# A packed-attention and SMeLU kernel on one core: casting loads, DMA transposes, no GpSimd compute, small matmuls on array tiles

## The chip, the cores and the metric

One core of one Trainium2 chip. The metric is the device time of one execution in microseconds. Times of kernels are medians of their runs. Stage times come from the trace of one profiled execution, counted from the start of its span, which is a little shorter than the timed run.

Engines: PE is TensorE (PEld its weight loads), DVE is VectorE, ACT is ScalarE, POOL is GpSimd, SP is SyncE.

## The reference

Eight batches (B) of eight heads (H), 576 tokens (S), head size 64 (D), 32 packing tokens per head. Cut to what matters:

```python
def sm_attn(qq, kk, vv):                       # softmax attention, scale 1/8
    ...
p_packed = sm_attn(p, k, v)                    # 32 packed rows per head
x = sm_attn(q, p_packed, p_packed)             # every token attends to 32 rows
x = x.transpose(0, 2, 1, 3).reshape(B * S, H * D)          # 4608 x 512
h = x @ w_in                                   # 512 x 2048
g = where(h >= 1, h, where(h <= -1, 0, (h + 1)**2 / 4))    # SMeLU
out = g @ w_out                                # 2048 x 512, float32
```

Both kernels use the same algebra: the second attention times `w_in` is regrouped as probabilities `A` times `M`, where `M` is the packed values times `w_in`.

## The kernel before

Each batch goes through: load k, v, q as float32; cast to bf16; transpose k and q on TensorE; scores, packed values, `M`, `A`; then a *stage* of 16 hidden tiles (`h`), into which the attention of the next batch, the output tiles (`o`) of the batch before and the casts of a later batch are woven. A scheduler orders the instructions of each engine.

```python
def load_tokens(src, b, tag, eng):             # float32, 4 tokens per partition, the rest apart
    t = stg.tile([P, H, NC4, D], f32, tag=tag, name=tag)          # one buffer per tensor
    eng.dma_start(...)
    r = stg.tile([REM, H, D], f32, tag=tag + "r", name=tag + "r")
    eng.dma_start(...)
...
def cast_steps(nm, b, engs): ...               # four casts per tensor, on the engines given
...
def scores(c0, n):                             # keys of two heads on all 128 rows,
    ... nc.tensor.matmul(sp[:, c, hp], kT[:, hp, ...], pT_blk[:, b, hp]...)   # p block-diagonal
...
def mk(g, f):                                  # M, on the whole array
    mp = psA.tile([P, FW], f32, tag="a", name="mp")
    for j in range(2):
        nc.tensor.matmul(mp, ppT[:, g, j], w_in_sb[:, 2 * g + j, ...], start=(j == 0), stop=(j == 1))
...
def hidden_tile(b, fi):
    ... # 4 matmuls of 288 columns into h
    nc.scalar.activation(r, hv, AF.Relu, bias=half, scale=0.5)
    if (fi * PB_SHARE) % 8 < PB_SHARE:         # 10 of 16 tiles
        nc.gpsimd.tensor_mul(u, r, r)
    else:
        nc.scalar.activation(u, r, AF.Square)
    nc.vector.scalar_tensor_tensor(dst, u, 1.0, hv, ALU.min, ALU.max)
...
run(cast_steps("k", 0, (V, A_, G_)))           # V, A_, G_: VectorE, ScalarE, GpSimd
...
for n in "kvq":
    run(cast_steps(n, 1, (V, A_, G_)))
```

The softmax here doesn't subtract the row's maximum and nothing guards it: scores larger than these inputs give would overflow.

## Time and profile before

334.59 us, median of 3 runs (333.87 to 337.23). From the trace, counted at the first matmul of `h` of each batch:

| stretch | us |
|---|---|
| start, to the first `h` | 37.1 |
| stage of batch 0 | 43.7 |
| stage of batch 1 | 31.0 |
| stages of batches 2 to 6 | 173.9 (34.8 each) |
| stage of batch 7, to the end of its last `h` | 26.7 |
| tail: the last output tiles | 21.6 |

First the page of the kernel before: busy time of TensorE; busy tenths of TensorE, of GpSimd and the granted TensorE clock in tenths of full speed, each in 40 equal slices of the span; and the shares of the chain that ended last.

```profile
PE 282.1 (84%) x1879; PEld 164.9 (49%) x1912; DVE 180.3 (54%) x324; ACT 206.7 (62%) x371; POOL 162.2 (49%) x190
...
PE   0274868887878998999899999999999999988894
...
POOL 4092237599858849237824693242433242434300
PEclk9998599997999999999999999999999999999999
...
PE 34%; issue 17%; POOL 16%; DMA 11%; DVE 10%; ACT 10%; POOLq 0%; SPq 0%; ACTq 0%
```

In the first thirteen slices (of 8.35 us each) TensorE never reaches 9 tenths, and GpSimd is at 8 or 9 tenths in five of the slices 9 to 14. The chain has 16% of GpSimd in it and 17% of "issue", so TensorE does not bound the whole run. Next, waits of the kernel before (engine, line, what was waited for: us in total, times, longest).

```profile
DVE hT L301 <- POOL u L298: 80.3, 66, 3.4
...
ACT kb_129 L125 <- DMA k<-in_k_dram: 8.6, 1, 8.6
...
DVE kb_129 L127 <- DMA k<-in_k_dram: 3.8, 1, 3.8
```

The last step of the hidden tiles (`hT`, on VectorE) waits 80 us in all for squares on GpSimd. ACT and VectorE each stand still once for a cast of batch 1's keys, which have not landed.

Last, pieces of TensorE's timeline of the kernel before (start, us, then what, and how many were merged). The last matmul of a group overlaps the first of the next, so the cost of a group is the difference of two starts, not the second column.

```profile
217.37 1.24 PE L321 MATMUL o<-w_out_sb,hT 128*128 128x512 bf16 x5
218.45 0.65 PE L288 MATMUL h<-A,M 128*128 128x288 bf16 x4
218.94 0.61 PE L166 MATMUL tp<-ident,kb_121 128*128 128x128 bf16 x8
...
221.19 0.40 PE L193 MATMUL sp<-pT_blk,kT 128*128 128x64 bf16 x8
221.64 0.81 PE L321 MATMUL o<-w_out_sb,hT 128*128 128x512 bf16 x3
...
228.52 0.84 PE L207 MATMUL pp<-vb_125,ex 128*128 128x320 bf16 x5
229.20 1.03 PE L321 MATMUL o<-w_out_sb,hT 128*128 128x512 bf16 x4
```

Five output matmuls take 1.08 us, 0.216 each; four of `h` 0.49. Eight scores (`sp`) take 0.45 here, but the next eight only 0.23 and the last four 0.12. Five packed matmuls (`pp`) take 0.68.

### The profile page before, as it was taken

What the parts mean: (1) busy time and instruction counts of PE and PEld (TensorE: products, weight loads), DVE (VectorE), ACT (ScalarE), POOL (GpSimd) and SP (SyncE); (2) the same over time, 40 slices, a digit from 0 to 9 for tenths busy, and PEclk for the clock granted to TensorE, in tenths of its full rate; (3) what the DMA queues carried; (4) which work ended last, traced back from release to release, by engine and by line L of the source; (5) the groups of instructions that cost most, each with busy time, mean ns of one, the idle gap of its engine ahead of it and who ended that gap; (6) DMA issues with size and microseconds to landing.
All of it is one profiled execution on the core that took longest, in us unless ns stands there. A gap on an engine that the chain in (4) does not pass through costs nothing.

```text
span 334.0 us, 5198 instructions
## 1 busy us (share of the span) xinstructions
PE 282.1 (84%) x1879; PEld 164.9 (49%) x1912; DVE 180.3 (54%) x324; ACT 206.7 (62%) x371; POOL 162.2 (49%) x190
## 2 busy tenths in 40 slices
PE   0274868887878998999899999999999999988894
PEld 0152345455444565557454655566546655444441
DVE  5332477564637764486457653767476638444300
ACT  2123745964668765966597747866977588666411
POOL 4092237599858849237824693242433242434300
PEclk9998599997999999999999999999999999999999
DMA  8999994577599595915740200000001200010031
GB/s 215 252 236 310 230 260 150 159 200 210 152 271 253 117 295 163 260 59 154 210 140 31 59 34 31 31 33 33 31 31 37 60 33 32 31 64 32 31 96 63
DMA packets 41689, 42.54 MB, mean 127 GB/s; under 512 B 12800, under 2 KB 35328, under 8 KB 41664
## 3 DMA queue, kind: packets, MB, share of 16 engines
q1 hardware_dynamic: 33472, 30.68, 31.6%
q0 software_dynamic: 8192, 11.54, 16.0%
q8 instruction: 15, 0.25, 0.3%
q14 instruction: 10, 0.08, 0.1%
HBM read 37.22 MB, written 9.44 MB: 140 GB/s over the span
## 4 chain that ended last, share of the span: by engine, by line
PE 34%; issue 17%; POOL 16%; DMA 11%; DVE 10%; ACT 10%; POOLq 0%; SPq 0%; ACTq 0%
PE o L321 15%; POOL u L298 9%; PE h L288 8%; DVE hT L301 5%; ACT r L295 4%; DMA kr<-in_k_dram 4%; PE mp L259 4%; DMA q<-in_q_dram 3%; DMA k<-in_k_dram 3%; DVE M L264 2%; PE tp L166 2%; DVE A L254 2%; ACT u L300 2%; POOL qb_131 L127 2%; POOL kb_121 L127 1%
## 5 line engine op out<-in xcount | busy, mean ns | idle before, releaser
L298 POOL TENSOR_TENSOR u<-r 128x576 f32<-128x576 f32 x80 | 91.7, 1148 | 126.8 <-ACT r L295 117.7
L301 DVE SCALAR_TENSOR_TENSOR hT<-u,h 128x576 bf16<-128x576 f32 x128 | 96.2, 752 | 94.7 <-POOL u L298 80.3
L321 PE MATMUL o<-w_out_sb,hT 128*128 128x512 bf16 x549 | 141.8, 380 | 1.5
L295 ACT ACTIVATE r<-h,half 128x576 f32<-128x576 f32 x128 | 94.7, 741 | 69.7 <-PE h L288 67.0
L288 PE MATMUL h<-A,M 128*128 128x288 bf16 x512 | 85.1, 290 | 16.0 <-DVE hT L301 15.4
L321 PEld LDWEIGHTS <-hT 128*128 128x128 bf16 x576 | 54.6, 98 | 49.8 <-DVE hT L301 0.6
L288 PEld LDWEIGHTS <-M 128*128 128x128 bf16 x512 | 49.5, 98 | 56.1 <-issue 20.6
L259 PE MATMUL mp<-w_in_sb,ppT 128*128 128x512 bf16 x122 | 36.9, 391 | 5.2 <-DVE M L264 3.1
L325 ACT COPY ob<-o 128x512 f32<-128x512 f32 x36 | 21.1, 587 | 20.2 <-PE o L321 20.0
L300 ACT ACTIVATE u<-r 128x576 f32<-128x576 f32 x48 | 32.9, 686 | 0.5
L264 DVE CAST M<-mp 128x512 bf16<-128x512 f32 x32 | 21.3, 684 | 9.1 <-PE mp L259 9.0
L254 DVE TENSOR_TENSOR A<-eT,rc 128x288 bf16<-128x288 bf16 x32 | 20.1, 632 | 6.3 <-ACT rc L253 6.2
L259 PEld LDWEIGHTS <-ppT 128*128 128x128 bf16 x128 | 12.8, 100 | 16.3 <-issue 10.6
L262 ACT CAST M<-mp 128x512 bf16<-128x512 f32 x32 | 18.7, 583 | 1.9 <-PE mp L259 1.6
L195 ACT ACTIVATE ex<-sp 128x512 bf16<-128x512 f32 (+1 forms) x24 | 12.3, 518 | 7.3 <-PE sp L193 7.2
L253 ACT ACTIVATE rc<-ln 128x288 f32<-128x288 f32 x32 | 14.1, 446 | 0.6
L167 DVE COPY qT<-tp 128x1024 bf16<-128x1024 bf16 x16 | 11.0, 688 | 4.8 <-PE tp L166 4.5
L251 ACT ACTIVATE ln<-sm 128x288 f32<-128x288 f32 x32 | 13.0, 411 | 0.1
L167 DVE COPY kT<-tp 128x1024 bf16<-128x1024 bf16 x16 | 11.0, 686 | 0.6 <-PE tp L166 0.4
L166 PE MATMUL tp<-ident,kb_121 128*128 128x128 bf16 x64 | 5.9, 242 | 6.2 <-DVE pT_blk L153 6.2
L193 PE MATMUL sp<-pT_blk,kT 128*128 128x64 bf16 x160 | 9.7, 200 | 0.9 <-ACT ex L195 0.6
L207 PEld LDWEIGHTS <-ex 128*128 128x128 bf16 x80 | 8.3, 104 | 3.7 <-issue 0.7
(152 smaller groups left out, 237.1 us busy)
## 6 DMA issues: line engine op xcount, KB each, us to landing
out_dram<-ob SPq DMA_DIRECT2D x32, 256.0 KB, 2.3
k<-in_k_dram SPq DMA_DIRECT2D x6, 1024.0 KB, 7.1
v<-in_v_dram SPq DMA_DIRECT2D x6, 1024.0 KB, 8.4
q<-in_q_dram SPq DMA_DIRECT2D x6, 1024.0 KB, 8.3
w_in_sb<-in_moe_w_in_dram POOLq DMA_DIRECT2D x4, 512.0 KB, 8.3
k<-in_k_dram POOLq DMA_DIRECT2D x2, 1024.0 KB, 9.5
v<-in_v_dram POOLq DMA_DIRECT2D x2, 1024.0 KB, 8.8
q<-in_q_dram POOLq DMA_DIRECT2D x2, 1024.0 KB, 9.9
```

Of the source, the lines that this page charges most:

```text
L167: nc.vector.tensor_copy(T[:, :, base + c0 * P:base + (c0 + 2) * P], tp.rearrange("p h c t -> p h (c t)"))
L254: nc.vector.tensor_mul(A[:, g, hf * HALF:(hf + 1) * HALF], eT, rc)
L259: nc.tensor.matmul(mp, ppT[:, g, j], w_in_sb[:, 2 * g + j, f * FW:(f + 1) * FW], start=(j == 0), stop=(j == 1))
L262: nc.scalar.copy(M[:, g, f * FW:(f + 1) * FW], mp)
L264: nc.vector.tensor_copy(M[:, g, f * FW:(f + 1) * FW], mp)
L288: nc.tensor.matmul(h[:, hf, :HALF], M[:, g, fi * P:(fi + 1) * P], A[:, g, hf * HALF:(hf + 1) * HALF], start=(g == 0), stop=(g == G - 1))
L295: nc.scalar.activation(r, hv, AF.Relu, bias=half, scale=0.5)
L298: nc.gpsimd.tensor_mul(u, r, r)
L300: nc.scalar.activation(u, r, AF.Square)
L301: nc.vector.scalar_tensor_tensor(dst, u, 1.0, hv, ALU.min, ALU.max)
L321: nc.tensor.matmul(o, hT[:, fi, i * P:(i + 1) * P], w_out_sb[:, fi, :], start=(fi == 0), stop=(fi == KF - 1))
L325: nc.scalar.copy(ob, o)
```

## The change

The intent is to free GpSimd and the casts' share of the other engines, and to take work off TensorE. Its parts:

1. Tokens are loaded by DMAs issued from GpSimd that cast float32 to bf16 on the way, six tokens on each of 96 partitions.
2. From batch 3 on, keys and queries are transposed by the DMA, SBUF to SBUF; before that on TensorE. One transpose turns two neighbouring chunks of a head: even chunks land on rows 0 to 63, odd ones on rows 64 to 127 (chunk parity).
3. Scores, packed values, probabilities and `M` run as many small matmuls on tiles of the array (64x96, 96x64, 64x32), instead of fewer ones on all of it with zero blocks.
4. The activation is a leaky ramp on ACT, a second pass on ACT or VectorE in turn, and a product on VectorE. GpSimd computes nothing but the identity matrix.
5. One pool of three two-bank buffers in PSUM (the memory that matmuls write to) for all but the output tiles, an order made by hand, and 25 matmuls on zeros at the start, meant to hold the clock.

```diff
 def load(nm, b):
+    t = stg.tile([TP, H, NC, D], bf16, tag=nm, name=nm)           # TP 96, NC 6, two buffers
+    nc.gpsimd.dma_start(t.rearrange("p h c d -> p h (c d)"), ...[b].rearrange("h (p c) d -> p h (c d)", c=NC))
...
+def xbar(b):
+    for nm, T in zip("kq", keys(b)):
+        nc.sync.dma_start_transpose(T.rearrange("p h e t -> p (h e) t"), tok[nm, b].rearrange("p h c d -> p (h c d)"))
...
 def scores(e0, n):
+    for e in range(n):
+        for g in range(G):
+            for a in range(Q):
+                for x in range(X):                                # row half = chunk parity
+                    r = slice(x * D, (x + 1) * D)
+                    nc.tensor.matmul(sp[:TP, x, e, g, a], kT[r, G * a + g, e0 + e], pT[r, b, g, a], ...)
...
 def mk(f):
+    for a in range(Q):
+        for g in range(G):
+            r = slice(g * D, (g + 1) * D)
+            nc.tensor.matmul(mp[a * NP:(a + 1) * NP, g], ppT[r, g, a], w_in_sb[r, a, ...], start=True, stop=True)
...
 def hidden_tile(b, fi, kind):
-    nc.scalar.activation(r, hv, AF.Relu, bias=half, scale=0.5)
-    ... nc.gpsimd.tensor_mul(u, r, r) / nc.scalar.activation(u, r, AF.Square) ...
-    nc.vector.scalar_tensor_tensor(dst, u, 1.0, hv, ALU.min, ALU.max)
+    nc.scalar.activation(x, hv, AF.Prelu, bias=-1.0, alpha=0.5)
+    # kind "W": nc.scalar.activation(t, x, AF.Relu, bias=1.0)
+    # kind "V": nc.vector.tensor_scalar(t, x, 1.0, 0.0, ALU.add, ALU.max)
+    nc.vector.scalar_tensor_tensor(dst, t, 1.0, t, ALU.min, ALU.mult)
...
+            a[26].append(lambda b=b: xbar(b + 2))                 # slot 26 of the 32 of a stage
```

## The prediction

> **What bounds the kernel now** (timeline, first matmul of `h` per batch).
> (a) 0 to 37 us: no hidden tile yet. TensorE is 11, 29 and 55% busy in the three ten-us windows from 0; casts wait for loads (8.6 us on ACT for one k in the waits view), and the granted clock falls to 0.50 in 30 to 40 us.
> (b) batch 0, 37 to 81 us: 43.7 us; GpSimd is 87% busy in 60 to 80 us with casts (1.04 us each) and squares (1.15 us, 80 of them); the chain of waits runs through both (POOL 16%).
> (c) batches 1 to 6, 81 to 286 us: 34.2 us each. TensorE is the limit: 97 to 99% busy in 200 to 280 us.
> (d) batch 7 (27 us) and the last five output tiles (21.5 us), nearly all TensorE.
>
> **TensorE per batch, before**, from start-to-start times in the timeline: 72 output matmuls at 0.216 = 15.5; 64 hidden at 0.122 = 7.8; 16 for `M` at 0.216 = 3.5; 40 transposes at 0.056 = 2.2; packed 1.4 plus 0.2; probabilities and sums 1.5; 20 scores at 0.033 = 0.7. Sum 32.8.
>
> **What the change does there.** Output and hidden matmuls (23.3 us) stay. `M` becomes 32 matmuls on 64-by-32 tiles, eight at a time. The Trainium skill ("TensorE: Matmul & The Clock Gate", Part 3) says such tiles run concurrently; not shown here yet. Estimate 1.3 us, saving 2.1. Probabilities likewise save 0.6. Transposes leave TensorE from batch 3 on, saving 2.2. But scores grow from 20 to 48 matmuls and packed from 10 to 48 plus 12, none with a full 128-column weight load: estimate 40 to 55 ns each, so 4.5 to 5 against 2.3. "TensorEngine Tiling (Array Packing)", Key Properties, says that changing the tiling mode drains the engine; about 20 changes per batch, estimate 1 to 2 us. Net: about 31.5 us, only 1 to 2 us less per batch.
>
> **Other engines.** ACT per batch: 16 first passes (0.74), 8 second passes (0.69), evacuations near 10: 27.6 as before, so 85% of the stage. VectorE 20 to 22. GpSimd computes nothing. ACT and TensorE now share three two-bank PSUM buffers; estimate 1 to 2 us of stalls per stage.
>
> **Where the gain lies.** Mostly in (a) and (b). No casts stand between landing and transposes, warming matmuls hold the clock: first `h` at about 26 us (saves 11), set by the first half of w_in behind k, v, q at 250 to 300 GB/s. Batch 0 stage 28 to 30 us (saves 14), set by ACT. Batch 1 about 34 (waiting for w_out and the third batch's q, around 66 to 73 us). Batches 2 to 6 about 32.5 each. Batch 7 24, tail 21.5.
> Sum: 26 + 29 + 34 + 162 + 24 + 21.5 = 296.5; I lean lower, as the placement looks tuned.
>
> **Predicted: 294 us, 8 in 10 between 276 and 312. Faster by over 2%: 0.90; within: 0.07; slower: 0.03.**
>
> **Right if** the profile shows: first `h` before 29 us; batch 0 under 32 us; no compute on POOL; steady stages 31 to 33 us with TensorE above 90% busy; eight `M` matmuls starting within about 0.4 us.
>
> **Wrong if**: the DMA transposes (590 KB each, issued about 9 us before the scores need them) take over 9 us, stalling every batch from 3 on (up to +30 us); small matmuls cost 80 ns each (+2 us per batch); mode changes cost more than 0.15 us; ACT, 85% loaded and in order, locks step with TensorE and becomes the limit; or tiles do not overlap, so `M` costs 6.9 us.

## More of the kernel before

Now the windows view, one stage per line (from and to, length; busy us and instructions of each engine; granted clock, DMA share, GB/s): batch 0, then batch 4.

```profile
37.06:80.76 43.70, 35.12 (x254) 20.63 (x258) 26.92 (x47) 27.58 (x48) 29.33 (x38) 0.93 0.83 208
182.37:218.45 36.08, 34.72 (x243) 20.73 (x246) 21.59 (x37) 25.08 (x47) 19.70 (x23) 1.00 0.11 37
```

In batch 4's stage TensorE is busy 34.7 of 36.1 us; in batch 0's, 35.1 of 43.7.

## The result, and the profile after

283.38 us, median of 4 runs (282.4 to 284.23), against 334.45 us for the kernel before in the same rounds. The ratio is 0.8459 (95% interval 0.841 to 0.8508). Ratios here are the mean time of one kernel's fast runs over that of the other's of the same rounds, so not quite the ratio of the medians quoted. A run more than 1.5% above the fastest of its kernel counts as slow and is left out of the ratios.

By stretch, from the two traces:

| stretch | before | predicted | after | after less before |
|---|---|---|---|---|
| start, to the first `h` | 37.1 | 26 | 24.7 | -12.4 |
| batch 0 | 43.7 | 29 | 28.7 | -15.0 |
| batch 1 | 31.0 | 34 | 32.7 | +1.7 |
| batches 2 to 6 | 173.9 | 162 | 150.8 | -23.2 |
| batch 7 | 26.7 | 24 | 21.0 | -5.7 |
| tail | 21.6 | 21.5 | 22.8 | +1.2 |
| span | 334.0 | 296.5 | 280.6 | -53.4 |

The page of the changed kernel, the same lines:

```profile
PE 257.3 (92%) x2545; PEld 142.1 (51%) x2545; DVE 175.9 (63%) x305; ACT 196.9 (70%) x309; POOL 27.1 (10%) x42
...
PE   6696885899999999989999999799999999999992
...
POOL 8411107002101200011001200000000000000000
PEclk9968899599999999999999999999999999999998
...
PE 70%; DVE 10%; DMA 9%; ACT 8%; issue 2%; DVEq 0%; ACTq 0%; POOLq 0%
```

TensorE is nearly full from slice 9 on (after 56 us) and is 70% of the chain. GpSimd left the chain; 9% of it is DMA. The waits of the changed kernel:

```profile
DVE hT L284 <- ACT t L293: 52.1, 44, 3.7
...
PEld L193 <- DMA kT<-k: 3.7, 3, 1.9
...
PE sp L193 <- DMA kT<-k: 2.7, 3, 1.6
```

The wait of `hT` is now for ACT, and costs nothing where TensorE is full; but three times TensorE and its weight loads wait for transposed keys (`kT`). The windows of the stages of batches 0, 4 and 5:

```profile
24.69:53.40 28.71, 20.92 (x296) 12.40 (x296) 22.49 (x41) 23.49 (x37) 7.72 (x12) 0.89 1.19 175
146.00:176.64 30.64, 30.64 (x305) 16.68 (x304) 20.83 (x34) 24.35 (x40) 2.31 (x3) 1.00 0.73 128
176.64:206.27 29.63, 27.85 (x291) 15.31 (x289) 19.85 (x33) 24.03 (x39) 0.00 (x0) 1.00 0.49 86
```

Batch 4's stage is TensorE from end to end. Batch 5's has one output tile less, but 1.8 us of idle TensorE. TensorE's timeline of the changed kernel shows where:

```profile
180.24 0.89 PE L193 MATMUL sp<-pT,kT 64*96 64x32 bf16 x32 [1.60 <-DMA kT<-k]
181.07 1.04 PE L312 MATMUL o<-w_out_sb,hT 128*128 128x512 bf16 x4
...
182.53 0.53 PE L193 MATMUL sp<-pT,kT 64*96 64x32 bf16 x16
182.99 1.04 PE L312 MATMUL o<-w_out_sb,hT 128*128 128x512 bf16 x4
...
184.88 0.94 PE L204 MATMUL pk<-ex,v 96*64 96x32 bf16 x48
185.75 0.45 PE L209 MATMUL pk<-ones_114,ex 96*128 96x2 bf16 x12
186.06 0.59 PE L312 MATMUL o<-w_out_sb,hT 128*128 128x512 bf16 x2
...
190.13 0.41 PE L246 MATMUL mp<-w_in_sb,ppT 64*32 64x512 bf16 x8
190.47 1.04 PE L312 MATMUL o<-w_out_sb,hT 128*128 128x512 bf16 x4
```

The scores waited 1.60 us for `kT`. The 48 scores then cost 0.83 + 0.46 us, the 48 packed matmuls with their 12 sums 1.18, and eight matmuls of `M` 0.34.

### The profile page after: what moved, and what is told of

It reads as the page before. It is cut to its first block, busy times and chain, and to the rows that moved or that the text cites. A ratio compares the mean times of both kernels' runs of the same rounds, so it can differ in the third digit from the quotient of the medians.

```text
span 280.6 us, 6146 instructions
## 1 busy us (share of the span) xinstructions
PE 257.3 (92%) x2545; PEld 142.1 (51%) x2545; DVE 175.9 (63%) x305; ACT 196.9 (70%) x309; POOL 27.1 (10%) x42
## 4 chain that ended last, share of the span: by engine, by line
PE 70%; DVE 10%; DMA 9%; ACT 8%; issue 2%; DVEq 0%; ACTq 0%; POOLq 0%
PE o L312 39%; PE h L273 17%; DMA kT<-k 6%; PE sp L193 4%; DVE hT L284 3%; PE mp L246 3%; DMA k<-in_k_dram 2%; PE pk L204 2%; ACT x L281 2%; ACT t L293 2%; DVE M L248 1%; ACT ln L235 1%; DVE pT L145 1%; DVE kT L183 1%; PE tp L179 1%
## 5 line engine op out<-in xcount | busy, mean ns | idle before, releaser
L284 DVE SCALAR_TENSOR_TENSOR hT<-t 128x576 bf16<-128x576 f32 x128 | 96.8, 757 | 55.4 <-ACT t L293 52.1
L281 ACT ACTIVATE x<-h 128x576 f32<-128x576 f32 x128 | 83.3, 651 | 36.5 <-PE h L273 29.4
L293 ACT ACTIVATE t<-x 128x576 f32<-128x576 f32 x64 | 43.9, 686 | 1.5
L287 DVE TENSOR_SCALAR t<-x 128x576 f32<-128x576 f32 x64 | 29.2, 456 | 6.0 <-ACT x L281 5.3
L195 ACT ACTIVATE ex<-sp 96x1024 bf16<-96x1024 f32 (+1 forms) x16 | 12.6, 803 | 15.6 <-PE sp L193 15.4
L248 DVE CAST M<-mp 128x1024 bf16<-128x1024 f32 x16 | 19.5, 1218 | 0.7 <-PE mp L246 0.7
L248 ACT CAST M<-mp 128x1024 bf16<-128x1024 f32 x16 | 16.1, 1007 | 0.2
L238 DVE SCALAR_TENSOR_TENSOR A<-eT,rs,rc 128x576 bf16<-128x576 bf16 x16 | 13.1, 816 | 5.1 <-ACT rc L237 5.1
L193 PE MATMUL sp<-pT,kT 64*96 64x32 bf16 x384 | 12.2, 197 | 3.0 <-DMA kT<-k 2.7
L246 PE MATMUL mp<-w_in_sb,ppT 64*32 64x512 bf16 x256 | 13.6, 407 | 0.9 <-ACT ln L235 0.8
```

Source lines behind the costliest of these rows:

```text
L193: nc.tensor.matmul(sp[:TP, x, e, g, a], kT[r, G * a + g, e0 + e], pT[r, b, g, a], start=True, stop=True)
L238: later(1, lambda: nc.vector.scalar_tensor_tensor(A[:, g], eT, rs[:, g, :1], rc, ALU.mult, ALU.mult))
L246: nc.tensor.matmul(mp[a * NP:(a + 1) * NP, g], ppT[r, g, a], w_in_sb[r, a, f * FW:(f + 1) * FW], start=True, stop=True)
L248: mcopy(f)(M[:, :, f * FW:(f + 1) * FW], mp)
L281: nc.scalar.activation(x, hv, AF.Prelu, bias=-1.0, alpha=0.5)
L284: nc.vector.scalar_tensor_tensor(dst, t, 1.0, t, ALU.min, ALU.mult)
```

## The experiments

The theory: in the steady stages TensorE is the limit, and a stage is the sum of its start-to-start times; in the start and in batch 0 the limit was casts and squares in in-order queues, and the landing of loads. The rival: steady stages are held by evacuations and PSUM buffers, and the early stretches by the loads or the clock alone. The experiments below are in the order of these questions.

### e1: transposes back on TensorE

```diff
-                a[26].append(lambda b=b: xbar(b + 2))
+                elif b > 1:
+                    a = spread([un[nm] for nm in EARLY], 3, 31)   # with kT0 qT0 kT1 qT1 in it
```

> The changed kernel (283.4 us), but batches 3 to 7 transpose keys and queries on TensorE again, as batches 1 and 2 do, and no DMA transpose is issued. Theory A (steady stages are bound by the sum of TensorE's start-to-start times): 48 transposes at about 0.043 us are 2.1 us a batch, five batches, +10 us, less about 3.5 us because the three stalls of 0.7 to 1.6 us on a late DMA transpose disappear: 288 to 293 us, steady stages up from 30.2 to 31.5 or more. Rival B (steady stages are bound by evacuations and PSUM buffers, so TensorE work is partly free): at most +2 us, or a gain, 280 to 285 us.

Measured: 290.35 us, ratio 0.8685 (0.8643 to 0.8727). The ratio is 0.023 above the changed kernel's first measurement (7.6 us of 334.79) and 0.018 above the later control of e11 (5.9 us). The windows of the stages of batches 4 and 5 of this run:

```profile
149.12:181.81 32.69, 32.04 (x347) 18.71 (x351) 23.95 (x42) 24.61 (x40) 2.31 (x3) 1.00 0.56 96
181.81:211.48 29.67, 29.17 (x334) 17.35 (x338) 22.46 (x42) 24.21 (x39) 0.00 (x0) 1.00 0.14 37
```

The stage of batch 4 grew from 30.6 to 32.7 us, by the 2.1 us expected. That of batch 5 hardly moved (29.6 to 29.7), because it lost its stall in exchange. Theory A holds: in batches 4 and 6, which had no stall, the added TensorE time is paid in full (2.05 us each). In batches 3 and 5 the stages are 1.7 us longer than the 27.95 us that they take without the stall (e12).

### e2: the same small matmuls, in an order that cannot overlap

```diff
-            for e in range(n):
-                for g in range(G):
-                    for a in range(Q):
-                        for x in range(X):
+            for x in range(X):
+                for e in range(n):
+                    for g in range(G):
+                        for a in range(Q):
...  # packed: g (column half) outermost instead of innermost
```

> The changed kernel with the same small matmuls in another order: scores with the row half (chunk parity) as the outermost loop, packed values with the column half as the outermost loop, so that neighbours share a half and cannot overlap. Theory A (halves run at the same time, which is why 48 scores take 1.04 us and 48 packed matmuls 0.86 us): each group of 48 about doubles, +1 us scores and +0.7 us packed per batch, 8 batches, total +8 to +13 us, 291 to 296 us. Rival B (one matmul leaves every 20 to 25 ns whatever its tile, an issue limit): groups unchanged, 282 to 285 us.

Measured: 298.90 us, ratio 0.8912 (0.8862 to 0.8963); at least 0.040 above the changed kernel, or 13 us. That is at or past the top of the expected range. The profiled execution is a slow one; in the stage of batch 4, from which these two lines of its TensorE timeline are, the granted clock was 1.00.

```profile
164.10 0.73 PE L193 MATMUL sp<-pT,kT 64*96 64x32 bf16 x16
...
166.87 1.59 PE L204 MATMUL pk<-ex,v 96*64 96x32 bf16 x48
```

The 16 scores take 0.73 us instead of 0.53, the 48 packed matmuls 1.59 instead of 0.94 (each with the latency of its last matmul, near 0.2 us, in it). The stage of batch 4 went from 30.6 to 32.1 us at the same clock. So halves of the array do run at the same time, and the order of the loops decides it: an issue limit would have shown no change. The starts show it too: in the changed kernel scores start in pairs, 4 ns and then 41 ns apart, and here mostly 45 ns apart each; packed matmuls 3 to 4 and then 28 to 29 ns, and here mostly 32. Every one of these matmuls has its own weight load, and in the changed kernel the loads start in pairs as well; no run separates the two. The 1.4 us of batch 4 in each of eight batches are 11 us, where the ratios give 13 to 15. What the rest is stays open: two stages of the profiled execution (batches 3 and 5) had a granted clock of 0.90 and 0.95, but a slow execution cannot settle it.

### e3: DMA transposes ten slots earlier

```diff
-                a[26].append(lambda b=b: xbar(b + 2))
+                a[16].append(lambda b=b: xbar(b + 2))
```

> The changed kernel with the DMA transposes issued at slot 16 of 32 of the stage before instead of slot 26. Theory A (TensorE stalls at the start of three stages because kT lands late, 0.7 to 1.6 us each): the stalls go, -2.5 to -3.5 us, 280 to 281 us. Rival B (the stall moves elsewhere, or the transposes then collide with token loads and output stores): within 1 us of 283.4.

Measured: 280.67 us, ratio 0.8385 (0.8349 to 0.842). No wait of TensorE for `kT` is left in the trace, and the stages of batches 3 and 5 are 28.0 us each, against 28.9 and 29.6. This profile is of a slow run, with a low clock before 60 us, so e12 below, a fast one, is what these stages rest on. Theory A holds.

### e4: no warming matmuls

```diff
 def warm(n):
-    o = psO.tile([P, d_model], f32, tag="o", name="o")
-    for _ in range(n):
-        nc.tensor.matmul(o, zeros[:, :P], zeros, start=True, stop=True)
+    return
```

> The changed kernel without the 25 warming matmuls on zeros. Theory A (they keep the granted clock up before the first hidden tile): the clock is half in 10 to 25 us, first h later by 1 to 2 us, total +1 to +3 us. Rival B (the start is set by the landing of k, v, q and w_in, and warming is free but useless): within 0.7 us of 283.4.

Measured: 281.85 us, ratio 0.8428 (0.8399 to 0.8456); first `h` at 24.4 us, against 24.7. That is 1.5 us below the changed kernel's first measurement, so theory A is out, and it is also below rival B's range: the warming matmuls bring nothing to the time here. The Trainium skill ("TensorE: Matmul & The Clock Gate", section "Why this matters for your kernels") advises keeping TensorE continuously busy for the full clock. The trace agrees in part: the 24 transposes of batch 0's keys, first in the changed kernel and then without warming, are

```profile
8.02 1.20 PE L179 MATMUL tp<-ident,k 96*128 96x96 bf16 x24 [1.41 <-DMA k<-in_k_dram]
7.89 2.10 PE L177 MATMUL tp<-ident,k 96*128 96x96 bf16 x24 [7.89 <-DMA k<-in_k_dram]
```

So warming did make the next matmuls faster, but it made the start no shorter: the first `h` waited for `A` (the last 1.06 us with the warming, 1.67 without), and TensorE had 13 more matmuls on zeros to do on the way. The recorded clock does not tell this: between 10 and 20 us it is 0.66 with the warming and 1.00 without, though without it the 48 scores of this stretch took 2.67 us, against 1.29 in a steady stage.

### e5 and e9: the kernel before, without squares on GpSimd

```diff
 def hidden_tile(b, fi):                        # in the kernel before
-    nc.scalar.activation(r, hv, AF.Relu, bias=half, scale=0.5)
-    ... nc.gpsimd.tensor_mul(u, r, r) / nc.scalar.activation(u, r, AF.Square) ...
-    nc.vector.scalar_tensor_tensor(dst, u, 1.0, hv, ALU.min, ALU.max)
+    nc.scalar.activation(x, hv, AF.Prelu, bias=-1.0, alpha=0.5)
+    if fi % 2 == 0:
+        nc.scalar.activation(t, x, AF.Relu, bias=1.0)
+    else:
+        nc.vector.tensor_scalar(t, x, 1.0, 0.0, ALU.add, ALU.max)
+    nc.vector.scalar_tensor_tensor(dst, t, 1.0, t, ALU.min, ALU.mult)
```

> The kernel before with one part of the change: the activation is computed as a leaky ramp on ACT, a second pass on ACT or VectorE in turn, and a product on VectorE, so GpSimd does casts only. Theory A (the squares on GpSimd, 1.15 us each behind casts of 1.04 us in one queue, held up the stages of batches 0 and 7, not the steady ones, which TensorE bounds): batch 0 from 43.7 to 36 to 39 us, batch 7 from 26.7 to 21 to 22, the rest within 1 us each, total 322 to 328. Rival B (batch 0 is held by loads and clock, and batch 7 by TensorE): no stage changes by over 1.5 us, 332 to 336 us.

Measured: 325.22 us in the median of all four runs; 321.04 and 324.31 in the two fast ones (326.13 counts as slow), ratio 0.9641 (0.9582 to 0.97). The profiled one took 1614 us: its 512-column matmuls lasted 1705 ns in the mean, against 380 ns, while the granted clock read 1.000. It stays unexplained. So the kernel was run once more.

> The same kernel as e5, whose profile fell in an execution of 1614 us with TensorE slow throughout and is of no use. Theory A (squares on GpSimd held batches 0 and 7): of the 12 us gained (ratio 0.964), 4 to 7 us lie in batch 0's stage (43.7 before), 4 to 6 us in batch 7's (26.7 before), and the steady stages stay within 1 us of 34.2 on average. Rival B (the gain is spread evenly over all stages): each stage 1.3 to 1.7 us shorter.

Measured: 321.63 us, ratio 0.9587 (0.9531 to 0.9644), profile fast. The windows line of its batch 0:

```profile
36.79:72.77 35.98, 31.11 (x221) 18.06 (x224) 26.39 (x46) 23.82 (x44) 15.45 (x21) 0.97 0.96 224
```

Batch 0 fell from 43.7 to 36.0 us, and batch 7 from 26.7 to 21.0, the value of the changed kernel. The six stages between lost 2.5 us together (205.0 to 202.5), the start 0.3. Theory A holds, with batch 0's share, 7.7 us, a little over the 4 to 7 expected. Part 4 of the change alone took 13 to 14 us off the kernel before. The edit replaces the whole activation; that it was the wait for GpSimd's squares which cost is read from the waits of the kernel before (80.3 us).

### e6: the kernel before, batch 1's casts all on GpSimd

```diff
-    run(cast_steps(n, 1, (V, A_, G_)))
+    run(cast_steps(n, 1, (G_, G_, G_)))
```

> The kernel before with one word changed: all casts of batch 1 go to GpSimd instead of VectorE, ACT and GpSimd in turn. Theory A (in the first 37 us VectorE and ACT stand in their queues behind casts that wait for batch 1's loads, 3.8 and 8.6 us, while batch 0's own work is ready): first h at 28 to 32 us instead of 37; what of it reaches the end depends on GpSimd, which then is fuller in batch 0's stage: total 326 to 333. Rival B (the start is set by the landing of batch 0's tokens and of w_in): first h within 2 us of 37, total 333 to 340.

Measured: 332.77 us, ratio 0.993 (0.989 to 0.997). The first `h` came at 31.7 us instead of 37.1: theory A's mechanism is right. VectorE's own timeline of the kernel before shows the queue: a reciprocal of batch 0 (second line) stands right behind a cast of batch 1's keys, and that cast waited 3.76 us for a load.

```profile
29.05 0.69 DVE L127 CAST kb_129<-k 128x1024 bf16<-128x1024 f32 x1 [3.76 <-DMA k<-in_k_dram]
29.66 0.16 DVE L211 RECIPROCAL rs<-pp 128x1 f32<-128x1 f32 x1
```

Of the 5.3 us gained there and 3.4 in batch 0, the stage of batch 1 took 5.0 back (31.0 to 36.0). The time moved by 0.7% only.

### e7: the first casts back on engines, and how the edit went wrong

```diff
+    for nm in "kvq":                           # batch 0 only, in the changed kernel
+        for i in range(2):
+            s = stg.tile([TP, 4, NC, D], f32, tag="raw", name="raw", bufs=3)
+            nc.gpsimd.dma_start(...)           # half of the tensor, as float32
+            (nc.scalar.copy if i else nc.vector.tensor_copy)(t[:, 4 * i:4 * i + 4], s)
```

> The changed kernel, but the tokens of batch 0 land as float32 (same queue, same order) and are cast by VectorE and ACT, half each. Theory A (a cast in the DMA saves only the cast's own time at the start, about 1.5 us for k and 1.5 us for q): first h 1.5 to 3.5 us later than 24.7, total 285 to 287 us. Rival B (casting DMAs are much faster to land as they write half the bytes): first h over 5 us later, total over 288 us.

Measured: 301.81 us, ratio 0.9013 (0.8967 to 0.9059); first `h` at 42.2 us. That is outside theory A's range, and rival B's reason is not shown either, because the edit made new waits. From its timeline:

```profile
19.33 1.82 ACTq L110 DMA_DIRECT2D p_raw<-in_p_dram  x4
...
27.15 0.29 DVE L144 CAST p_nat<-p_raw 128x256 bf16<-128x256 f32 x1 [7.38 <-DMA p_raw<-in_p_dram]
```

With three staging halves, GpSimd could issue q's loads only after k's casts (at 11.5 us); and the issue of half of p stood on ACT's queue behind casts until 19.3 us, so that p was there at 27 us. It says nothing of casting loads, but shows again what e6 shows: an issue or a cast that waits holds up all that stands behind it in its queue.

### e10: the same, mended

```diff
+    raw0 = hT...bitcast(f32)...                # room for all of k, v, q of batch 0
+    for n, nm in enumerate("kvq"):
+        nc.gpsimd.dma_start(raw0[:, n]..., ...)           # float32
-            (nc.sync, nc.scalar)[g].dma_start(p_raw...)
+            nc.sync.dma_start(p_raw...)
...  # casts on VectorE and ACT, half each, just before their use; identity made before the loads
```

> e7 mended: its first h came 17.5 us late because three staging halves made the load queue wait for casts, and the issue of half of p stood in ACT's queue behind casts. Here batch 0 lands as float32 into room for all of it, p is issued from SyncE, nothing waits for a buffer; the casts run on VectorE and ACT, half each. Theory A (a cast in the DMA saves the cast's own time, 0.95 to 1.5 us on each of k, v, q): first h 26 to 29 us against 24.7, total 284.5 to 288 us. Rival B (casting DMAs land much sooner): first h over 30 us, total over 289.

Measured: 293.11 us, ratio 0.8731 (0.8678 to 0.8784), against 284.84 us and 0.8510 for the control of the same rounds: 8.3 us by the medians, 7.4 us by the ratios, which leave out the one slow run of e10. First `h` at 33.0 us. The time from issue to landing of batch 0's k, v and q in the changed kernel, in this order, and the page's GB/s in 40 slices:

```profile
DMA to landing us min/median/max: 6.7/6.7/6.7
DMA to landing us min/median/max: 8.7/8.7/8.7
DMA to landing us min/median/max: 10.9/10.9/10.9
...
GB/s 102 206 212 204 205 204 87 202 204 155 166 109 152 210 153 40 121 164 189 103 143 169 182 118 36 167 84 36 37 176 73 37 40 46 68 39 39 75 77 76
```

The same of e10, its three float32 loads in one line:

```profile
DMA to landing us min/median/max: 8.6/13.5/17.8
...
GB/s 134 222 210 212 202 207 171 134 204 156 159 157 121 152 205 100 41 179 174 183 69 156 198 134 36 141 97 40 36 120 134 58 38 36 49 63 37 72 74 72
```

Adding the times of issue, the casting loads landed at 8.0, 10.9 and 13.8 us, 2.9 us apart; the float32 loads at 10.1, 15.9 and 21.0 us, 5.8 and 5.1 us apart. Each reads 1.18 MB from HBM. The GB/s, which count the bytes written, are nearly the same in both in slices 2 to 6 (202 to 222). So in these loads the bytes written set the pace, and casting on the way about doubles the rate at which the source is read. Rival B's numbers hold. But not all of the loss comes from this: p, in e10 issued from one queue, landed at 16.0 us and its cast on VectorE waited 1.94 us for it, the casts of v and q took their places in the queues, and the granted clock was half in slices 2 to 4. If p's wait is taken off the 8.3 us by which the first `h` came later (33.0 against 24.7), the casting loads are worth about 6 us of the start, landing and cast time together; this split is worked out, not shown.

### e8: batch 0's second pass on the idle GpSimd

```diff
-            later(1, lambda: nc.scalar.activation(t, x, AF.Relu, bias=1.0))
+            # batch 0 only:
+            later(1, lambda: nc.gpsimd.tensor_scalar(t, x, 1.0, 0.0, ALU.add, ALU.max))
```

> The changed kernel with the second pass of every other hidden tile of batch 0 on the idle GpSimd instead of ACT (8 passes of 0.69 us). Theory A (batch 0's stage, 28.7 us with TensorE 59 to 85% busy, is bound by ACT and VectorE, each 73 to 95% busy): the stage shrinks by 1.5 to 4 us, total 280 to 282 us. Rival B (it is bound by the landing of batch 1's tokens, of w_out and by the latency of the chain from tile to tile): within 1 us of 28.7, total 282.5 to 284.5 us.

Measured: 307.72 us, ratio 0.9191 (0.9159 to 0.9223): 24 us slower than the changed kernel, and nearly all of it is in batch 0's stage (28.7 to 52.7 us). GpSimd's timeline of this run:

```profile
38.03 0.57 POOL L348 DMA_DIRECT2D p_nat<-in_p_dram  x1 [4.45 <-DMA w_out_sb<-in_moe_w_out_dram]
...
46.06 4.28 POOL L294 TENSOR_SCALAR t<-x 128x576 f32<-128x576 f32 x2
```

GpSimd was idle, but its queue was not empty: loads of p and of batch 2 stood in it, each issue waiting for an earlier load to land, so the first pass ran at 46 us; and one pass takes 2.1 us there. Neither theory is tested by it. What bounds batch 0's stage in the changed kernel stays open.

### e11 and e12: a control, and e3 with e4

```diff
-                a[26].append(lambda b=b: xbar(b + 2))
+                a[16].append(lambda b=b: xbar(b + 2))
...  # and warm() returns at once
```

> The changed kernel itself, as control on this chip for e12: 282 to 285 us, ratio 0.841 to 0.851, stages as in its first profile (28.7, 32.7, 31.0, 28.8, 30.6, 29.6, 30.6, 21.0 us).

> The changed kernel with the DMA transposes issued at slot 16 and without warming matmuls (e3 and e4 together). Theory A (the stalls on late transposes are the only part that costs; warming is worth nothing): 279.5 to 281 us, 2.5 to 4 us below the control of the same chip. Rival B (e3's gain was the chip's, not the kernel's): within 1 us of the control.

Measured: the control took 284.84 us, ratio 0.8510 (0.8473 to 0.8547), its stages as expected. The combined kernel took 279.71 us, ratio 0.8356 (0.8324 to 0.8388); the intervals do not touch. It is 1.8% faster than the changed kernel in the same rounds, beats both kernels, and its gain of 5.1 us is more than expected. The windows line of its stage of batch 5, from a fast run:

```profile
175.65:203.60 27.95, 27.33 (x286) 15.30 (x289) 19.84 (x33) 24.01 (x39) 0.00 (x0) 1.00 0.39 82
```

Batch 5's stage is 28.0 us, against 29.6; its wait for `kT` is gone. Theory A holds for the stalls. The spans of the two profiles differ by 3.2 us (281.1 and 277.9), of which 2.8 lie in the stages of batches 2 to 6. The control's profiled run is its fastest (282.90 us); why the medians differ by more stays open.

## Why the prediction was right, and where it was off

The range (276 to 312) and the direction held: 283.38 us. The point, 294, was 10.6 us too high. One of the prediction's own tests failed: the steady stages were to take 31 to 33 us, and those of batches 2 to 6 took 28.9 to 31.0.

- **Right: most of the early gain.** The start and batch 0 were to give 11 and 14 us; they gave 12.4 and 15.0. e9 shows that 7.7 us of batch 0's came with the activation that takes the squares off GpSimd. e6 shows the queues behind casts in the start, though removing them alone returned little at the end. e10 shows that the float32 loads with casts would cost 7 to 8 us. Where the other 7.3 us of batch 0 come from stays open, and the prediction's "set by ACT" for that stage is not shown: ACT is busy for 23.5 of its 28.7 us, VectorE for 22.5.
- **Wrong in its reason: what sets the first `h`.** The prediction said "set by the first half of w_in behind k, v, q at 250 to 300 GB/s". From one landing to the next the casting loads read 1.18 MB in 2.9 us, about 407 GB/s; with the 6.7 us of the first one, k, v, q and half of w_in (5.6 MB) had landed at 19.2 us, 294 GB/s from the start. So the landing itself was estimated well, but it did not set the time: `M`'s first matmuls ran at 20.95 us right behind the probabilities, without a wait for w_in; after them the first `h` waited for the sums and `A`. The number was near partly by luck: the chain of batch 0's attention was ready 1.8 us after that landing. That "warming matmuls hold the clock" added nothing to the time (e4).
- **Right: the steady stages are TensorE's sum.** For batch 4 (five output tiles) the start-to-start times of the kernel before add up to about 34.5 us: 17.3 for outputs, 7.8 for `h`, 3.5 for `M`, 2.2 for transposes, 3.7 for the rest. Those of the changed kernel: 17.3, 7.8, 1.4 for `M`, 0.5 for probabilities and 0.5 for sums, 1.3 for scores, 1.2 for packed values, which is 30.0, against 30.6 measured. e1 added to the sum and e3 took a wait away, and the stage followed.
- **Mis-sized: scores and packed matmuls.** The term was "estimate 40 to 55 ns each, so 4.5 to 5"; it measured 2.5 us per batch, hardly more than the 2.3 that the prediction gave the kernel before. The prediction let `M`'s tiles overlap, but costed scores and packed matmuls as a row, one after another. e2 shows that they overlap by halves, too. And "estimate 1 to 2 us of stalls per stage" was too much: batch 4 has none, batch 5 1.8 us. The first of these terms is 2.0 to 2.5 us in each of five stages, 10 to 12 us, which is the size of the whole miss of batches 2 to 6 (162 predicted, 150.8 measured); with the stalls and the mode changes (below) the over-estimates are more than the miss, so they do not account for it exactly; the saving is 4.6 us per stage, not the 2.3 that 34.8 less 32.5 made.
- **Batch 7** was over-estimated by 3 us. In e9 it is 21.0 us as well, so the activation with squares on GpSimd is what made it 26.7.
- **The feared wait was real but small.** From issue to landing the DMA transposes of keys took 5.1 to 6.8 us and those of queries 4.9 to 8.7, not over 9; but they were issued so late that TensorE or its weight loads waited in three stages, up to 1.9 us. e3 and e12 got that back. In e12 the first pair took 16.3 and 16.8 us, but issued so early that nothing waited for it.
- **Tiles at once.** The Trainium skill ("TensorE: Matmul & The Clock Gate", Part 3) says that matmuls on different tiles run concurrently. The trace agrees: eight matmuls of `M` with 512 columns cost 0.34 us together, where four on the whole array cost 0.86.
- **Mode changes.** The skill ("TensorEngine Tiling (Array Packing)", Key Properties) says that a change of tiling mode drains TensorE. No run isolates this. The sum above leaves at most 0.6 us per stage for all of it, not the 1 to 2 us estimated.

## What to carry to other kernels

Before costing a set of small matmuls, see which tiles of the array neighbours in the order use: here two that use different halves cost hardly more than one (45 ns a pair of scores, against 45 each in e2's order), and the loop order alone was worth 13 us or more. List what each in-order queue holds in the start: a cast or a DMA issue that waits for a load holds up everything behind it, on any engine, and an idle engine may have a full queue. Where TensorE is the limit from end to end, sum its start-to-start times: a microsecond added there shows, and a transfer that arrives just late costs as much. Check a recorded clock against the durations of like matmuls: in e4's start and in e5 it read 1.00 while matmuls took twice and 4.5 times as long as usual.

## What the Trainium skill lacked or had wrong

- "DMA: Bandwidth & Descriptors", Rules for kernel authors, says that a casting DMA is issued from GpSimd; no page says what the cast is worth. Here float32 loads of 1.18 MB landed 5.1 and 5.8 us apart, loads cast to bf16 2.9 us apart: the bytes written set the pace, 203 to 231 GB/s of them in these loads (1.18 MB in 5.1 and 5.8 us, 0.59 MB in 2.9 us).
- The same page, Latency and other measured facts, gives 261 GB/s and more for DMA transposes. Here one of the keys, 590 KB (96 x 3072 bf16), took 5.1 to 6.8 us from issue to landing, about 110 GB/s end to end at the median of 5.4 us. This is not the page's measure: the issuing instruction alone held SyncE's queue for 3.0 to 3.6 us of it, and the next transpose was issued only after it.
- "TensorE: Matmul & The Clock Gate", Part 1, gives a floor of about 25 ns from start to start for small matmuls. In the trace 32 scores on alternating halves started within 0.70 us, 23 ns apart in the mean, and neighbouring matmuls of `M` on different tiles 3 to 4 ns apart: the floor does not hold across tiles. Part 1 states it without this exception; Part 3 of the page has it, with about 4 ns from tile to tile. The 12 sums, all on the same rows and columns, did start 25 to 26 ns apart, save the first gap of 38.
- The same page advises work to keep the clock up; 25 warming matmuls sped up the first transposes (1.20 against 2.10 us) but bought nothing in the time (e4), and the recorded clock was lower with them (0.66 between 10 and 20 us) than without (1.00).
- The same page's Part 1 warns that records of the clock can be unreliable. No page has the size seen here: one whole execution (e5) took 1614 us with matmuls 4.5 times as long as usual, at a granted clock recorded as 1.000.
